# Two token tiles of a gated layer by seven block products in place of eight, behind the layer before it

## The chip, the cores and the metric

The kernel runs on one core of one Trainium2 chip. The metric is the device time of one execution in microseconds, the median of several runs.

## What is computed

Three stages follow one another. A state-space scan over 768 steps (4 batches, 8 heads) gives 3072 tokens of 256 values. Block one is a feed-forward layer of 2048 columns with an ELU. Block two gates two projections of 1024 columns and multiplies the product by two matrices:

```python
x = scan(x, a, B, C).reshape(3072, 256)
h = x @ w_in                                   # 256 -> 2048
x = np.where(h > 0, h, np.exp(np.minimum(h, 0)) - 1) @ w_out   # -> 256
a, b = x @ w1, x @ w2                          # 256 -> 1024 each
out = ((a * b) @ w3) @ w_out2                  # -> 1024 -> 256
```

Inputs and outputs are fp32. The large products run on a rounded fp32 form (float32r): each operand is split into a high part and a low part (what rounding left), and one product is the sum of three matmuls.

## The kernel before

Tokens lie along the free dimension in 6 tiles of 512 (`TT`); features lie on the 128 partitions. The scan works on 24 chunks of 128 steps, four for each tile. Chunks 0 to 3 are done first, step by step; the others come in pairs. `unit_u(k)` computes the products of C with B and the new states of two chunks, `unit_y(k)` their output, which becomes the columns of `xT` for tile k // 4, as high and low part. `at_prep` (L394) is the scan on VectorE that turns decays into the mask L.

Block one goes tile by tile in 8 units of 256 columns. `unit_a(t, n)` makes 12 matmuls into a room of two PSUM banks; then ScalarE takes exp and relu, VectorE joins them with h (L608), and ScalarE and VectorE split the result g into parts. `unit_b(t, n)` multiplies g by `w_out` with 12 matmuls into two accumulators (`acc_b`); for the first four units of tile 0, with plain fp32 words, it needs four matmuls. After the eighth, `split_x2` splits x2 into parts. Tiles 0 to 2 write x2 to DRAM and read it back later (`x2_stored`, `x2_back`).

Block two goes tile by tile in 8 blocks m of 128 columns. `unit_c(t, m)` makes 12 matmuls into a room of two banks, one for each of w1 and w2; ScalarE copies the first (L704), VectorE multiplies it by the second (L706), ScalarE and VectorE split the product p (L713, L122). `unit_d(t, m)` makes 6 matmuls with wp, the product of w3 and the last matrix, which `unit_w` computes beforehand with 192 matmuls of 256 columns.

Every large product is this one:

```python
def mm3(out, whi, wlo, xhi, xlo, first, last, **kw):
    T.matmul(out, wlo, xhi, start=first, stop=False, **kw)
    T.matmul(out, whi, xlo, start=False, stop=False, **kw)
    T.matmul(out, whi, xhi, start=False, stop=last, **kw)
```

Weights come from DRAM as 64-bit words in pieces of 512 KB; a class `Piece` turns each into fp32 with one instruction of ScalarE and two of VectorE, and then into a high part (ScalarE) and a low part (`take_lo`, L122, on VectorE or GpSimd). All loads and stores are issued by SyncE.

The order of all work on every engine is written out by hand: `ORDER` is a string of letters, each of which runs the next waiting step of its kind (`a`, `b`, `c`, `d`, `w`, `u`, `y` are the units; most other letters are single instructions of ScalarE, VectorE or GpSimd), and `in_order` keeps each engine to it. In this string block two of tiles 0, 3, 1, 2 is mixed with the scan and block one of tiles 4 and 5, and the first four chunks have a list of their own, `FIRST_SCAN`. PSUM has 8 banks: three rooms of two banks (`ps_w`) and two accumulators (`ps_a`), which block one and block two share.

Of the kernel before, what the change touches and what calls it, by code (L numbers as in the profile page):

```python
# [35 lines left out]
sbxkrijNsuhKaWkDHDjIKbxtHtiryhIsNbzkzMYYMKXiHahXIjkiaxKrLHsbBxIrLNahsBijbVxRraSsCShCTCTuxCi1brsDahtViaxDtrVVbxsrLyshBiaM  # L36
MzzXYYkbXxLrPKBkHbshIKNiHuhIkaDDjNtbtxirKjsyhkHibMIMzXzYbNYhKkHXiIaKjNkHLIaxKrBkNLHbxIsjrBNKahsSiShwTxTk1jirbKHsfIHFjakh
INRwxKrCNkCjsbHCfIKjFHaCNihIkaxiNjKrkLwxsBrKjbsHfIHFkIuNKhaDtDjNtwkxirKsjaHkfKIHFbkxINKrswhkNjiKyHfIHFbMjzINzYMYbLXhkjNB
iuXhKwkPDjDttbKHfkIHiIyFKwMzMzYXYLXaHLBfHIFRaxBIrLCwxCsrBCshbNCfiFaSkNSThT3jiaxKjkNrKbx1sHrIbNkhsjiHahKNkjiHaxIKrNIHbsjk
xIjbKhkKriHasHIhINbxirsajNkhKHibxIjkrKbHsIhuicDtDtbmnpqcSST3Tcmnpqcmndmncpqdmncpqcmndmndpqcpqcmndmncpqdmncpqdmncpqdmncpq  # L40
oO2cddpqcpmqnmndmndpqcpqcmndmncpqdmndpqcpqdmncpoOq2ymndzMz3YcYpqLMcXmBnXLPdmBncpqRdmnCupCqdDcptDtqcmnymndzMzMYcYXpqXLdLm
BCdnpBqCcpqdmnuOop2cDtDtqdmcnpqamndxrcpsqhdmidpncqpqcmnamnyxrdzMzsdpYhqaYpiqdxLrdBsaOo2axrsbbhixahribxsrbshiahiaxrsbxrsb
hiuhbDiDbttySSTTzczYYcmnpqcmnpqcmncmndmndpqcpqdmnapqdxrcpsqhdmidncpqamnpqaxrsdxhdriaOos2axrsbahixbrxsbhriahsibxrsahibxrs
bhihigGSTeSTEmnmpncmqpnqpqcmnpqdmndpqddccmnpqcmnpqdmndpqddoO
"""
TILES_OF_C = (0, 3, 1, 2, 4, 5)
SPILL = 3
VECTOR_LO = 16
PIECES = [(("w_in", "w_out")[k == "o"], "iiiooioiiiiooooo"[:n].count(k)) for n, k in enumerate("iiiooioiiiiooooo")] + [("wo2", m) for m in range(4)] + [("w3", m) for m in range(16)] + [
    (k, m) for k in ("w2", "w1") for m in range(4)]  # L50

PLAIN = 4

FIRST_SCAN = ["a0", "l0", "a1", "l1", "c0", "u0", "m0", "a2", "l2", "c1", "u1", "p0", "d0", "d1", "a3", "m1", "l3", "y0", "x0",
              "c2", "u2", "d2", "m2", "kjK", "y1", "x1", "c3", "u3", "d3", "HI", "kjK", "m3", "y2", "x2", "h0", "HkjI", "y3",
              "x3", "h1", "n0", "n1", "n2", "n3"]

# [5 lines left out]
def kernel(  # L63
# [27 lines left out]
    ps_w = ctx.enter_context(tc.tile_pool(name="ps_w", bufs=3, space=bass.MemoryType.PSUM))  # L91
    ps_a = ctx.enter_context(tc.tile_pool(name="ps_a", bufs=1, space=bass.MemoryType.PSUM))
# [7 lines left out]
    sel = const.tile([SUB * CPT, CPT, SUB, R], F32R, name="sel")  # L100
# [51 lines left out]
    class Piece:  # L152
# [89 lines left out]
    def cols_of(ws):  # L242
        return lambda i: [w[:, :, i * 256:i * 256 + 256] for w in ws]

    def rows_of(ws):
        return lambda i: [w[:, 2 * i:2 * i + 2] for w in ws]
# [18 lines left out]
    def half_cols(ws, name):  # L265
        def dst(i):
            if not ws:
                ws.extend(four(name, name, [P, F2]))
            return [[w[k][:, i * 256:i * 256 + 256] for k in range(2)] for w in ws]
        return dst  # L270

    def w3_dst(i):
# [42 lines left out]

    def at_first():
# [483 lines left out]
    for p in queue[3:8]:  # L800
        p.load()
# [88 lines left out]
```

## Time and profile before

| | |
|---|---|
| three runs | 548.15, 549.25, 549.32 us (median 549.25) |
| profiled execution | 548.17 us, its span 546.5 us |
| busy | TensorE 531.1, VectorE 341.3, ScalarE 270.2, GpSimd 69.1 us |
| moved | 45.58 MB read, 6.39 MB written |
| mean granted clock of TensorE | 0.999 of 2.4 GHz |

The span runs from the first to the last instruction; the device time has some work around it. In the profile's rows PE is TensorE's matmul, PEld its weight load, DVE is VectorE, ACT ScalarE, POOL GpSimd and SP SyncE. `L394` is a line of the kernel. A row of a stretch gives its start and end, its length, the busy time and the count of instructions of PE, PEld, DVE, ACT and POOL, then the granted clock, the DMA engines' share and GB/s. A row of a timeline gives start, length, engine, line, instruction and count, and in brackets the idle time of that engine before it and what ended it.

### The profile page before, as it was taken

What the parts mean: (1) busy time and instruction counts of PE and PEld (TensorE: products, weight loads), DVE (VectorE), ACT (ScalarE), POOL (GpSimd) and SP (SyncE); (2) the same over time, 40 slices, a digit from 0 to 9 for tenths busy, and PEclk for the clock granted to TensorE, in tenths of its full rate; (3) what the DMA queues carried; (4) which work ended last, traced back from release to release, by engine and by line L of the source; (5) the groups of instructions that cost most, each with busy time, mean ns of one, the idle gap of its engine ahead of it and who ended that gap; (6) DMA issues with size and microseconds to landing.
All of it is one profiled execution on the core that took longest, in us unless ns stands there. A gap on an engine that the chain in (4) does not pass through costs nothing.

```text
span 546.5 us, 10462 instructions
## 1 busy us (share of the span) xinstructions
PE 531.1 (97%) x4420; PEld 427.6 (78%) x4420; DVE 341.3 (62%) x487; ACT 270.2 (49%) x374; POOL 69.1 (13%) x84
## 2 busy tenths in 40 slices
PE   6888899999999999999999999999999999999997
PEld 3646588878888888888888887888888788887885
DVE  6698798999999798874333346644635444454233
ACT  2668666566766358863323232224555234655222
POOL 2420002035452270000000002010000000000000
PEclk9999999999999999999999999999999999999999
DMA  8993652257524639140001025310000000100001
GB/s 300 321 311 122 189 193 79 64 168 229 178 89 143 206 127 340 44 154 1 1 0 38 2 78 175 118 40 0 33 27 0 2 1 1 39 1 0 1 0 40
DMA packets 27167, 52.65 MB, mean 96 GB/s; under 512 B 2192, under 2 KB 10512, under 8 KB 27120
## 3 DMA queue, kind: packets, MB, share of 16 engines
q1 hardware_dynamic: 27120, 51.98, 28.7%
q8 instruction: 35, 0.57, 0.4%
q14 instruction: 12, 0.10, 0.1%
HBM read 45.58 MB, written 6.39 MB: 95 GB/s over the span
## 4 chain that ended last, share of the span: by engine, by line
PE 91%; DMA 3%; ACT 2%; DVE 1%; SPq 1%; issue 1%; DVEq 0%; ACTq 0%
PE ab L290 8%; PE ab L292 8%; PE ab L291 8%; PE acc_b L290 7%; PE h L290 7%; PE acc_b L291 7%; PE h L291 7%; PE h L292 7%; PE acc_b L292 7%; PE acc_d L290 4%; PE acc_d L292 4%; PE acc_d L291 4%; DMA raw_wo<-in_w_out 2%; PE wp L290 1%; PE wp L292 1%; PE wp L291 1%
## 5 line engine op out<-in xcount | busy, mean ns | idle before, releaser
L290 PE MATMUL h<-xTh,w_in_lo 128*128 128x512 f32 (+1 forms) x196 | 76.6, 391 | 2.5 <-DVE w_in_lo L122 2.3
L706 DVE TENSOR_TENSOR pa<-pa,ab 128x512 f32<-128x512 f32 x48 | 32.8, 685 | 71.7 <-ACT pa L704 71.5
L608 DVE SCALAR_TENSOR_TENSOR e<-e,h 128x1024 f32<-128x1024 f32 x44 | 53.5, 1217 | 37.5 <-ACT e L603 37.4
L291 PE MATMUL h<-xTl,w_in_hi 128*128 128x512 f32 (+1 forms) x196 | 75.6, 386 | 0.1
L292 PE MATMUL h<-xTh,w_in_hi 128*128 128x512 f32 (+1 forms) x196 | 75.5, 385 | 0.0
L290 PE MATMUL ab<-x2h,w 128*128 128x512 f32 x192 | 75.2, 392 | 0.0
L291 PE MATMUL ab<-x2l,w 128*128 128x512 f32 x192 | 74.7, 389 | 0.0
L292 PE MATMUL ab<-x2h,w 128*128 128x512 f32 x192 | 74.7, 389 | 0.0
L704 ACT COPY pa<-ab 128x512 f32<-128x512 f32 x48 | 28.1, 588 | 91.5 <-PE ab L292 91.5
L290 PE MATMUL acc_b<-g,w_out_lo 128*128 128x512 f32 x176 | 69.3, 394 | 1.7 <-DVE w_out_lo L122 1.7
L601 ACT ACTIVATE e<-h 128x1024 f32<-128x1024 f32 x48 | 49.3, 1027 | 43.3 <-PE h L292 43.1
L122 DVE TENSOR_TENSOR g<-e,g 128x1024 fp32r<-128x1024 f32 x44 | 56.7, 1288 | 21.3 <-ACT g L612 21.1
L291 PE MATMUL acc_b<-g,w_out_hi 128*128 128x512 f32 x176 | 68.7, 390 | 0.8 <-DVE g L122 0.8
L292 PE MATMUL acc_b<-g,w_out_hi 128*128 128x512 f32 x176 | 68.5, 389 | 0.0
L612 ACT CAST g<-e 128x1024 fp32r<-128x1024 f32 x44 | 46.3, 1053 | 35.4 <-PE acc_b L292 32.6
L603 ACT ACTIVATE e<-e 128x1024 f32<-128x1024 f32 x48 | 50.9, 1061 | 1.1
L122 DVE TENSOR_TENSOR p<-pa,p 128x512 fp32r<-128x512 f32 x48 | 33.6, 700 | 28.3 <-ACT p L713 27.9
L713 ACT CAST p<-pa 128x512 fp32r<-128x512 f32 x48 | 29.8, 622 | 41.0 <-PE acc_d L292 28.1
L400 POOL TENSOR_TENSOR xbc<-xbc,L 128x128 f32<-128x128 f32 x24 | 13.2, 548 | 256.3 <-DVE L L394 240.6
L290 PEld LDWEIGHTS h<-xTh,w_in_lo 128*128 128x128 f32 x196 | 36.8, 188 | 11.2 <-issue 1.8
L292 PEld LDWEIGHTS h<-xTh,w_in_hi 128*128 128x128 f32 x196 | 36.8, 188 | 7.5
L291 PEld LDWEIGHTS h<-xTl,w_in_hi 128*128 128x128 f32 x196 | 36.8, 188 | 7.3 <-DVE xTl L122 0.3
(119 smaller groups left out, 880.5 us busy)
## 6 DMA issues: line engine op xcount, KB each, us to landing
xbc<-in_xc SPq DMA_DIRECT2D x24, 512.0 KB, 5.8
raw_wc<-in_w3t SPq DMA_DIRECT2D x16, 512.0 KB, 4.3
L<-a_cut SPq DMA_DIRECT2D x40, 128.0 KB, 3.5
raw_wi<-in_w_in SPq DMA_DIRECT2D x8, 512.0 KB, 8.2
raw_wo<-in_w_out SPq DMA_DIRECT2D x8, 512.0 KB, 6.7
out_t<-o SPq DMA_DIRECT2D x12, 256.0 KB, 2.0
raw_wq<-in_wo SPq DMA_DIRECT2D x4, 512.0 KB, 7.2
raw_wb<-in_w SPq DMA_DIRECT2D x4, 512.0 KB, 6.2
```

Source lines behind the costliest of these rows:

```text
L122: eng.tensor_tensor(out=lo, in0=raw, in1=hi.bitcast(F32), op=ALU.subtract)
L290: T.matmul(out, wlo, xhi, start=first, stop=False, **kw)
L291: T.matmul(out, whi, xlo, start=False, stop=False, **kw)
L292: T.matmul(out, whi, xhi, start=False, stop=last, **kw)
L400: G.tensor_tensor(out=c["bd"], in0=c["bn"], in1=c["L"][:, :, R - 1:R].to_broadcast([P, NH, N]), op=ALU.mult)
L601: A.activation(e, h, AF.Exp)
L603: A.activation(e, e, AF.Relu, scale=-1.0, bias=1.0)
L608: V.scalar_tensor_tensor(out=gt[t, n] if plain else e, in0=e, scalar=-1.0, in1=h, op0=ALU.mult, op1=ALU.max)
L612: A.copy(g[:, 0], e)
L704: A.copy(e, h[:, 0])
L706: V.tensor_tensor(out=e, in0=e, in1=h[:, 1], op=ALU.mult)
L713: A.copy(p[:, 0], e)
```

## The change

For tiles 2q and 2q+1 together, the two weights and the two halves of the 256 features make a 2 x 2 product of blocks: (w1, w2) by (tile 2q, tile 2q+1). It takes eight block products; the change takes seven, by a form of Strassen's method, with more sums around them.

- The weights' sums are made once for each 256 columns (`gated_sums`, on GpSimd, four sums for each of four pieces) from the fp32 words, and seven operands of each are split into parts (`gated_hi`).
- The tokens' sums are made for each pair (`x2_sums`, `x2_last`, on GpSimd, four of 128x512), and seven operands are split (`operand`: ScalarE, then VectorE). x2 is no longer split at its end but kept whole (`x2_made`); tiles 0 to 3 go to DRAM and back, one tensor each.
- `by_product` issues one of seven products (letters `c e g G E ( )`). Products are added up in four rooms of one bank: two that blocks m take in turn (`p` in the order), `p_A` and `p_E`. A bank is read between two products that are added to it: `kept_1`, `kept_5` and `kept_2` are copies by ScalarE, `sum_11`, `sum_22` and `sum_12` sums by VectorE, `gate_1` and `gate_2` the two gating products on VectorE. `gate_parts` splits p as before.
- Block two of all tiles stands behind the scan and block one in `ORDER`. Its operands use the places of w_in and w_out, its weights the places of the scan's loads. PSUM is handed over in two steps: three rooms of two banks become four rooms of one bank and two accumulators, so block two has four accumulators.
- The first four chunks are now in `ORDER` too, in pairs (`first_cb`, `first_u`, `first_y`); the first half of a unit of tile 0 (`half_a`) is issued ahead for two units. Pieces of w_in and w_out load in another order, and L has four buffers in place of three.

The core of the diff:

```diff
-NMMXKajXkHLjaPxNIBKjNkrLaMxsBXjKrNbkxRXjrsCNjCKbWjCsHCjkjIujKNWkaDKtHkjNIxDaKrtkHsNjbxIKrkLHjysBWIzMazYMhKXkHYKXaxLrPINB
+094AAlU75AlCCACl5Cl5jk5U!KNjkJHKJ6IDN6HjD8N66IQj8D8NDj8kzQNzkYjYzKvzXYjYKaXkHKjvIxMkkarKMkHasxPIrLNbxLBrXsBKXbjRHWNICsMu
...
-TILES_OF_C = (0, 3, 1, 2, 4, 5)
-SPILL = 3
+SPILL = 4
...
-    def unit_c(t, m):
-        h = banks(f"ab{t}_{m}")
-        for k in range(2):
-            c_products(h, t, m, k)
-        yield "m"
-        yield from c_parts(t, m, h)
...
+    def x2_sums(q):
+        (b11, b21), (b12, b22) = ([x2[2 * q + j][:, k] for k in range(2)] for j in range(2))
+        t1, t3 = (att.tile([P, TT], F32, tag="pr", name=f"t{q}_{j}", bufs=2) for j in range(2))
+        G.tensor_tensor(out=t1, in0=b12, in1=b11, op=ALU.subtract)
+        G.tensor_tensor(out=t3, in0=b22, in1=b12, op=ALU.subtract)
+        G.tensor_tensor(out=b12, in0=b22, in1=t1, op=ALU.subtract)
+        later("~", x2_last, q, b11, b21, b12)
+        ops_x[q] = []
+        for n, raw in enumerate((b11, t1, b21, b12, t3, b22, b11)):
+            later("@", operand, q, n, raw)
...
+    def by_product(l, q, m):
+        n = "cegGE()".index(l)
...
+        o = ops_x[q][n]
+        whi, wlo = (v[:, m % 2 * P:m % 2 * P + P] for v in ops_w[m // 2][(0, 4, 1, 5, 6, 2, 3)[n]])
+        ps = rooms["E"] if l in "e(" else rooms["A"] if l == "g" else rooms[m % 2]
+        mm3(ps, whi, wlo, o[:, 0], o[:, 1], l in "ceg", l in "g()", skip_group_check=True)
+        s = mid.setdefault((q, m), {})
+        kind, step = {"c": ("m", kept_1), "e": ("n", kept_5), "g": ("[", sum_11), "G": ("]", kept_2),
+                      "E": ("{", sum_22), "(": ("}", sum_12), ")": (">", gate_1)}[l]
+        later(kind, step, s, q, m)
...
+    def sum_22(s, q, m):
+        V.tensor_tensor(out=s["two"][:, 1], in0=s["p5"], in1=rooms[m % 2], op=ALU.add)
...
+    def gate_1(s, q, m):
+        V.tensor_tensor(out=s["two"][:, 0], in0=s["two"][:, 0], in1=rooms[m % 2], op=ALU.mult)
+        later("p", gate_parts, 2 * q, m, s["two"][:, 0])
```

**The order on TensorE at the start.** Before, where `aw` are the decays of one chunk, `f` its room, and `xbc` its loaded columns:

```order
L382 MATMUL aw_135<-a_hl,sel 128x512 x2
L382 MATMUL aw_140<-a_hl,sel 128x512 x2
L416 MATMUL f_145<-xbc_104 64x128 x8
L451 MATMUL f_145<-xbc_104 32x64 x8
L382 MATMUL aw_165<-a_hl,sel 128x512 x2
L416 MATMUL f_170<-xbc_106 64x128 x8
L451 MATMUL f_170<-xbc_106 32x64 x8
L382 MATMUL aw_193<-a_hl,sel 128x512 x2
```

And in the changed kernel, where two chunks share each room of decays:

```order
L450 MATMUL f_138<-a_hl,sel 128x512 x4
L484 MATMUL f_136<-xbc_111 64x128 x4
L484 MATMUL f_137<-xbc_113 64x128 x4
L484 MATMUL f_136<-xbc_111 64x128 x4
L484 MATMUL f_137<-xbc_113 64x128 x4
L450 MATMUL acc_f<-a_hl,sel 128x512 x4
L484 MATMUL f_138<-xbc_117 64x128 x4
L484 MATMUL acc_f<-xbc_119 64x128 x4
```

The products of C and B (L416 before, L484 now) and those of the states stood chunk by chunk between the decays; now those of two chunks alternate, and all four chunks' come before the states' products.

**The order on VectorE in block two.** Before, where `pa` is the copied w1 half, `ab` the room, and `p` the parts of the gated product:

```order
L706 TENSOR_TENSOR pa_4_3159<-pa_4_3159,ab_4_3093 128x512
L706 TENSOR_TENSOR pa_5_3163<-pa_5_3163,ab_5_3114 128x512
L706 TENSOR_TENSOR pa_6_3172<-pa_6_3172,ab_6_3144 128x512
L122 TENSOR_TENSOR p_4_3181<-pa_4_3159,p_4_3181 128x512
L122 TENSOR_TENSOR p_5_3197<-pa_5_3163,p_5_3197 128x512
L706 TENSOR_TENSOR pa_7_3213<-pa_7_3213,ab_7_3184 128x512
L706 TENSOR_TENSOR pa_0_3222<-pa_0_3222,ab_0_3200 128x512
L122 TENSOR_TENSOR p_6_3238<-pa_6_3172,p_6_3238 128x512
```

And in the changed kernel, in the second pair, for block 3 and part of block 4 (`p_3795` and `p_3796` are the two rooms that blocks take in turn, `p_A` and `p_E` the other two; `p_3843` and `u_3891` are copies that ScalarE kept; `c` holds what becomes the two tiles' gated products; L795 is `sum_22`, L792 `sum_11`, L798 `sum_12`, L801 `gate_2`, L805 `gate_1`, L128 the low part):

```order
L795 TENSOR_TENSOR c_3_4386<-p_3843,p_3796 128x512
L792 TENSOR_TENSOR c_3_4386<-c_3_4386,p_A 128x512
L801 TENSOR_TENSOR c_3_4386<-c_3_4386,u_3891 128x512
L805 TENSOR_TENSOR c_3_4386<-c_3_4386,p_3796 128x512
L128 TENSOR_TENSOR p_3_4469<-c_3_4386,p_3_4469 128x512
L128 TENSOR_TENSOR p_3_4479<-c_3_4386,p_3_4479 128x512
L798 TENSOR_TENSOR u_3891<-u_3891,p_E 128x512
L795 TENSOR_TENSOR c_4_4447<-p_3843,p_3795 128x512
L801 TENSOR_TENSOR c_4_4447<-c_4_4447,u_3891 128x512
L128 TENSOR_TENSOR p_4_4503<-c_4_4447,p_4_4503 128x512
```

One product and one low part for each tile and block, two and two for a pair, became three sums, two products and two low parts for the pair; five of the seven stand in the order between products that TensorE adds to the same rooms.

## Rows read from the trace of the kernel before

**Rows 1.** The page, its first part: busy time, share of the span, instructions.
```profile
PE 531.1 (97%) x4420; PEld 427.6 (78%) x4420; DVE 341.3 (62%) x487; ACT 270.2 (49%) x374; POOL 69.1 (13%) x84
```

**Rows 2.** Stretches of the span; columns as told in the section on the profile.
```profile
0.00:19.30 19.30, 13.68 (x281) 8.36 (x281) 12.55 (x23) 5.87 (x12) 5.86 (x17) 1.00 0.92 327
19.30:80.10 60.80, 55.69 (x621) 38.15 (x622) 50.42 (x80) 42.48 (x61) 8.96 (x17) 1.00 0.71 219
80.10:243.40 163.30, 163.30 (x1533) 136.88 (x1537) 144.65 (x201) 108.69 (x146) 47.75 (x42) 1.00 0.46 152
243.40:323.50 80.10, 80.10 (x420) 65.99 (x428) 30.95 (x48) 24.35 (x41) 0.00 (x0) 1.00 0.04 13
323.50:502.00 178.50, 178.50 (x1411) 146.03 (x1412) 87.53 (x118) 76.57 (x95) 6.54 (x9) 1.00 0.11 37
```

**Rows 3.** The page, its fourth part: the chain that ended last, by engine.
```profile
PE 91%; DMA 3%; ACT 2%; DVE 1%; SPq 1%; issue 1%; DVEq 0%; ACTq 0%
```

**Rows 4.** Timeline of TensorE, 256 to 262 us: first and last of 28 starts.
```profile
255.78 0.39 PE L292 MATMUL ab<-x2h,w 128*128 128x512 f32 x1
...
261.90 0.39 PE L292 MATMUL ab<-x2h,w 128*128 128x512 f32 x1
```

**Rows 5.** Timeline of TensorE, 0 to 75 us: start, length, instruction, idle time before it.
```profile
6.70 1.13 PE L416 MATMUL f<-xbc 32*64 32x128 f32 x16
...
19.29 0.38 PE L290 MATMUL h<-xTh,w_in_lo 128*128 128x256 f32 x1 [0.22 <-POOL w_in_lo L122]
...
24.29 0.40 PE L290 MATMUL h<-xTh,w_in_lo 128*128 128x512 f32 x1
...
28.07 0.47 PE L290 MATMUL h<-xTh,w_in_lo 128*128 128x512 f32 x1 [0.87 <-DVE w_in_lo L122]
...
44.42 0.47 PE L290 MATMUL h<-xTh,w_in_lo 128*128 128x512 f32 x1 [1.38 <-DVE w_in_lo L122]
...
61.48 0.69 PE L416 MATMUL s<-xbc 32*64 32x128 f32 x32
...
67.21 0.50 PE L290 MATMUL acc_b<-g,w_out_lo 128*128 128x512 f32 x1 [1.67 <-DVE w_out_lo L122]
```

**Rows 6.** Timeline at the end of block one and at the last output.
```profile
504.49 1.22 DVE L122 TENSOR_TENSOR g<-e,g 128x1024 fp32r<-128x1024 f32 x1 [1.49 <-ACT g L612]
...
505.76 0.50 PE L291 MATMUL acc_b<-g,w_out_hi 128*128 128x512 f32 x1 [0.76 <-DVE g L122]
...
506.10 0.40 PE L292 MATMUL acc_b<-g,w_out_hi 128*128 128x512 f32 x1
...
542.18 0.39 PE L292 MATMUL acc_d<-p,wp_hi 128*128 128x512 f32 x1
...
542.66 0.59 ACT L736 COPY o<-acc_d 128x512 f32<-128x512 f32 x1 [3.48 <-PE acc_d L292]
```

**Rows 7.** Groups by line and form: count, busy us and mean ns, idle before.
```profile
L122 DVE TENSOR_TENSOR p<-pa,p 128x512 fp32r<-128x512 f32 x48 | 33.6, 700 | 28.3 <-ACT p L713 27.9
...
L706 DVE TENSOR_TENSOR pa<-pa,ab 128x512 f32<-128x512 f32 x48 | 32.8, 685 | 71.7 <-ACT pa L704 71.5
L713 ACT CAST p<-pa 128x512 fp32r<-128x512 f32 x48 | 29.8, 622 | 41.0 <-PE acc_d L292 28.1 <-DVE pa L706 10.7 <-DVE p L122 2.2
L704 ACT COPY pa<-ab 128x512 f32<-128x512 f32 x48 | 28.1, 588 | 91.5 <-PE ab L292 91.5
```

**Rows 8.** Timeline of VectorE and GpSimd, 128 to 134 us.
```profile
128.78 1.21 DVE L394 TENSOR_TENSOR_SCAN L<-L,eye 128x512 f32<-128x512 f32 x1
...
130.45 1.63 POOL L122 TENSOR_TENSOR w<-raw_wc,w 128x512 fp32r<-128x512 f32 x1 [2.49 <-ACT w L194]
...
130.83 2.33 DVE L394 TENSOR_TENSOR_SCAN L<-L,eye 128x512 f32<-128x512 f32 x1
...
132.04 1.34 POOL L400 TENSOR_TENSOR xbc<-xbc,L 128x128 f32<-128x128 f32 x1
...
133.09 1.19 DVE L608 SCALAR_TENSOR_TENSOR e<-e,h 128x1024 f32<-128x1024 f32 x1
```

More of the change, by code (lines that the diff above doesn't have):

```diff
@@ L199, in los @@
                 take_lo(self.lo, l, w, h)
-    w_in_s = pair([P, 2, F1], "w_in")
-    w_out_s = pair([P, F1 // P, DM], "w_out")
+    NA, NC = F1 // P // 2, F2 // P
+    w_in_s, w_out_s = ([wts.tile([P, 2, 2, 256], F32R, tag=f"{name}{n}", name=f"{name}{n}") for n in range(NA)]
+                       for name in ("w_in", "w_out"))
     wp_s = pair([P, F2 // P, DM], "wp")
-    wo2_s, w1_s, w2_s = [], [], []
+    wo2_s = []
     w3_st = {}
@@ L240, in blocks, with parts_at, acc_of @@
                 for f in range(0, F2, P) for i in range(0, F2, 512)]
[L242 to L246, printed above, removed]
+    def parts_at(ws):
+        return lambda i: [ws[i][:, p] for p in range(2)]
+    acc_f = ps_f.tile([P, 2, TT], F32, name="acc_f")
+    accs = []
+    def acc_of(i, other=0):
+        if not accs:
+            pool = sums(two, "ps_a", 1, "right")
+            accs.extend(pool.tile([P, TT], F32, name=f"acc{j}") for j in range(2))
+        return accs[2 * other + i]
     words = []
@@ L263, in wo2_dst, with slot @@
         return [w[i // 2][:, 2 * (i % 2):2 * (i % 2) + 2] for w in wo2_s]
[L265 to L270, printed above, removed]
+    slots = []
+    def slot(n):
+        if n // 2 >= len(slots):
+            j = len(slots)
+            if j < 8:
+                new = [wts.tile([P, 4, 256], F32R, tag=f"w{2 - j // 4}_{j % 4}", name=f"s{j}")]
+            elif j < 12:
+                new = [att.tile([P, 4, 256], F32R, tag="xbc", name=f"s{j}", bufs=4)]
+            else:
+                both = [att.tile([P, 2, 256], F32R, tag="L", name=f"s{j}_{k}", bufs=4) for k in range(2)]
+                slots.append(both)
+                return slot(n)
+            slots.append([new[0][:, :2], new[0][:, 2:]])
+            return slot(n)
+        return slots[n // 2][n % 2]
@@ L695, in ended_c @@
[L695 to L708 removed]
+        nc.sync.dma_start(x2_dram[t], x2.pop(t))
+    x2_dram = tc.dram_tile([SPILL, P, 2, TT], F32, name="x2_dram")
@@ new lines, in x2_last, with operand @@
+    def x2_last(q, b11, b21, t2):
+        G.tensor_tensor(out=b11, in0=b21, in1=t2, op=ALU.subtract)
+    def operand(q, n, raw):
+        o = wts.tile([P, 2, TT], F32R, tag=f"{('w_in', 'w_out')[q % 2]}{n}", name=f"x{q}_{n}")
+        ops_x[q].append(o)
+        A.copy(o[:, 0], raw)
+        yield "#"
+        take_lo(V, o[:, 1], raw, o[:, 0])
+    rooms = {}
+    mid = {}
+    def by_product(l, q, m):
+        n = "cegGE()".index(l)
+        if not rooms:
+            pool = sums(six, "ps_c", 1, "left")
+            rooms.update({k: pool.tile([P, TT], F32, name=f"p_{k}") for k in (0, 1, "A", "E")})
+            accs.extend(pool.tile([P, TT], F32, name=f"acc{j}") for j in (2, 3))
+        o = ops_x[q][n]
[6 more added lines that the diff above has]
+        later(kind, step, s, q, m)
+        if l in "E(":
+            s["ready"] = s.get("ready", 0) + 1
+            if s["ready"] == 2:
+                later("<", gate_2, s, q, m)
@@ new lines, in halves_of, with kept_1, kept_5, kept_2 @@
+    def halves_of(name, tag, m):
+        if name not in rooms:
+            rooms[name] = wts.tile([P, 2, TT], F32, tag=tag, name=name)
+        return rooms[name][:, m % 2]
+    def kept_1(s, q, m):
+        s["two"] = tmp(f"c{q}_{m}")
+        A.copy(s["two"][:, 0], rooms[m % 2])
+    def kept_5(s, q, m):
+        s["p5"] = halves_of("p5", f"w_in{NA - 1}", m)
+        A.copy(s["p5"], rooms["E"])
+    def kept_2(s, q, m):
+        s["u2"] = halves_of("u2", f"w_out{NA - 1}", m)
+        A.copy(s["u2"], rooms[m % 2])
@@ new lines, in unit_d, with copied @@
+        for i, kind, cs in ((0, "o", slice(0, TT)), (1, "O", slice(0, TT // 2)), (1, "o", slice(TT // 2, TT))):
+            later(kind, copied, t, i, tmp(f"o{t}_{kind}{i}")[:, 0, cs], cs, A if kind == "O" else nc.sync)
+    copies = []
+    def copied(t, i, o, cs, queue):
+        (A.copy if i == 1 and cs.start == 0 else V.tensor_copy)(o, acc_of(i, t % 2)[:, cs])
+        if queue:
+            stored(queue, t, i, o, cs)
+            return
+        copies.append((nc.sync, t, i, o, cs))
+        if len(copies) == 2:
+            later("2", lambda: [stored(*copies.pop(0)) for _ in range(2)] and None)
```

346 lines of the change are left out of this document (169 added, 177 removed).

## Prediction

> **What bounds the kernel now.** I read the busy shares first, then the stretches, then the chain of waits, and only then single instructions. TensorE is busy 531.1 of 546.5 us, VectorE 341.3, ScalarE 270.2, GpSimd 69.1 [rows 1]. A busy share is an average, so the stretches decide: from 80.1 us to 502 us TensorE is busy in every microsecond (163.30 of 163.30, 80.10 of 80.10, 178.50 of 178.50), at a granted clock of 1.00, which is its 2.4 GHz level; before 80.1 us it is idle for 5.6 and 5.1 us [rows 2]. VectorE takes 144.65 of 163.3 us (89%) in the middle of block one and 30.95 of 80.1 us (39%) where only block two runs [rows 2]. So another engine's work costs nothing as long as TensorE doesn't have to wait for it, and this holds at 89%. The chain of waits says the same: 91% of it is TensorE [rows 3]. In a dense stretch 27 matmuls of 512 columns go by between the starts at 255.78 and 261.90 us: 6.12/27 = 0.2267 us each [rows 4]. The 0.39 us that a row prints is not its cost, since matmuls overlap.
>
> **The change, part by part.**
>
> *Products taken away.* For two token tiles and one 128-column block m of block two, the kernel issued 2 tiles x 2 weights x 2 halves x 3 parts = 24 matmuls; now 7 products x 3 = 21. There are 3 pairs x 8 blocks: 504 in place of 576. The order of instructions bears this out (288 into the two alternating banks, 72 into p_A, 144 into p_E). 72 x 0.2267 = **-16.3 us**, all of it on the path, since TensorE had no gap there. The 288 matmuls of the output product stay. Nothing here can take this away; what follows can only add to it or eat it.
>
> *The start.* The first four chunks are now issued in pairs. One chunk alone takes 1.13 us for its 16 products of C and B, a pair takes 0.69 us for 32 [rows 5]. The first w_in product stands at 19.29 us [rows 5]; I keep that time, because the same four scans, the same masked products and one weight piece are ahead of it on VectorE's queue in either order. What changes is what follows: units 0 and 1 of block one now come with nothing of the scan between them and would both be done at 19.3 + 2 x 2.72 = 24.7 us, where the second of them ended at 24.29 + 12 x 0.2267 = 27.0 [rows 5]. That is 2.3 us. From there to 80.1 us the old TensorE is idle for 5.1 us [rows 2], of which 0.87, 1.38 and 1.67 are waits for VectorE's low parts [rows 5], and it loses about 1 us more in first matmuls that start slowly after a wait (0.34 in place of 0.23 [rows 6]). Pieces of w_in and w_out are now loaded in turn, so the low parts of w_out can come sooner. All of it gone would be -8 us, none of it 0. VectorE's 63 us of work in the first 80.1 [rows 2] would then have to fit into 72, so some waits will stay. I take **-5 us**; a load that comes late could cost up to 3 us instead.
>
> *Block one without block two between.* Three u units, four y units and tiles 4 and 5 of block one move ahead of all of block two, so VectorE gets no relief until about 340 us. Its work outside the gating is at most 341.3 - 33.6 - 32.8 = 275 us [rows 1, 7]; the 16 new low parts of the summed weights and the operands that are made early are at most 30 instructions, 21 us at 0.70. 296 of 340 us is 87%, no more than the 89% under which TensorE never waited [rows 2, 7]. Cost 0. The cover is VectorE's 13%; were it gone, each missing microsecond would stand on the path. The x2 traffic falls from 6 stores and 6 loads to 4 and 4. The eight loads of w1 and w2 keep their number and now wait on SyncE's queue behind the last chunks of the scan; nothing of block one is queued behind them that is due soon. Also 0.
>
> *A gap that goes.* At 505.76 us TensorE resumes after 0.76 us without work, on the last g of tile 5 [rows 6]. Now 12 us of other units are issued between unit 7 of the last tile and its second product: **-0.8 us**.
>
> *Gating in block two.* For each pair and m ScalarE had 4 instructions (2 copies, 2 casts), VectorE 4. Now ScalarE has 5 and VectorE 7, all 128x512. VectorE: 24 x 7 x 0.70 = 118 us, with the operands of the later pairs about 130 of 180 us, or 72% [rows 7]. Share is not the risk; the banks are. A product's bank is added to again after it has been read, so 168 product groups of 0.68 us each wait for a copy or a sum. The trace has no such wait; the nearest rows price its parts. A reader starts 0.25 us after the last matmul's slot (542.18 + 0.23 to 542.66) and TensorE resumes 0.05 us after the vector instruction (504.49 + 1.22 to 505.76) [rows 6]. So a round trip is 0.25 + 0.59 + 0.05 = 0.89 us over ScalarE and 0.99 over VectorE, if nothing is queued ahead. In the new order I counted what TensorE is given meanwhile: 0.68 us in 4 places, 1.36 us in 44, 2.05 us or more in the other 116. The 4 lose up to 0.3 us each. The 44 lose nothing with a free engine, and 0.2 to 0.3 us with one instruction ahead. I walked the second pair by hand, from the first product of block 4 to the outputs of block 3, by these prices: VectorE's four sums and products of block 3 end 5.7 us after that start, its two low parts at 6.4 and 7.6, and the output products that need them are due at 8.2 and 9.5. No wait there. I take 1.2 us for the 4, a third of the 44 at 0.2 us, and nothing for the chain to the output product, about **+4 us** in all. Bounds: 0.5 us (all but the 4 covered) and 12 us (every one of the 48 at 0.25).
>
> *GpSimd's new work.* 16 sums of weights and 12 of x2 tiles. In the old trace a VectorE scan of 1.21 us takes 2.33 us when a GpSimd subtraction of 1.63 us began just before it: it ends 1.1 us after that subtraction does, as if it had begun there [rows 8]. The sums of weights lie in block one, where VectorE has the slack. Of the 12 x2 sums 8 lie where block one ends and the first pair begins; what they could hold up there is rival B, and in the sum I take 0. The Trainium skill (the page "SBUF — State Buffer", section "Who interferes with whom") makes this a rule against the change: a VectorE instruction with both inputs in SBUF and a GpSimd instruction that reads SBUF shut each other out for the whole instruction. The trace agrees (2.33 in place of 1.21 us [rows 8]). If the rule struck at every added x2 sum, the sum would be B's 536 us; without it, 531.
>
> **Sum.** 546.5 - 16.3 - 5 - 0.8 + 4 = 528.4 us of span. The profiled execution took 548.17 us, 1.67 more than its span: 530.1. It stands 1.1 us under the median of the three runs (549.25), so on that scale **531 us**. A difference under 0.2% (1.1 us) can't be told from none here.
>
> **Rivals.**
>
> *A. The gating falls behind (10%).* If an instruction stands ahead on VectorE at most of the 44 places, and the late output products then hold the p tiles, the waits cost 12 to 19 us and nearly all of the 16.3 is given back: 539 to 546 us. For it: four one-bank rooms where three two-bank rooms were, and 72% load in place of 39%. Against it: the walk above, and 116 of the 164 covers being over 2 us.
>
> *B. The lock on the switch (10%).* Eight GpSimd sums at 1.1 us hold VectorE back by up to 9 us while it must also make the last g tiles and 14 operands; TensorE has 12 us of other work there, so some 5 us come through: 536 us. For it: the scan that was held up [rows 8]. Against it: an instruction that reads its second input from PSUM shows no such stretch (L608 at 133.09, 1.19 us beside a GpSimd product [rows 8]), and the four GpSimd sums of one pair needn't all meet a low part.
>
> *C. Slower than before (6%).* Without any wait in block two the sum is 531 - 4 = 527 us. To pass 549.25 block two would have to wait 22 us, 0.93 us per pair and m. A wait with 1.36 us of cover over VectorE loses 0.99 + 0.69k - 1.36 us with k instructions ahead; with two such places per pair and m, k = 1.2 on average is the point from which the change loses. Then VectorE's fixed order, not TensorE, would set the pace, with all 7 instructions of a block strung on the bank's chain. The walk shows k near 0 in the one place tried, so I hold this improbable.
>
> That the change doesn't do what it says is shut out by the order of instructions: 504 matmuls stand there in place of 576. No difference within 0.2% (2%) is only the narrow strip between A and C.
>
> **How the numbers follow.** The forecast has 72%. Its own range takes the start and the waits to their bounds: 546.5 - 16.3 - 8 - 0.8 + 0.5 + 2.8 = 525 us, and 546.5 - 16.3 - 0 - 0.8 + 8 + 2.8 = 540 (waits at two thirds of their bound, as both ends together are unlikely; 2.8 is 1.67 + 1.1). B lies in it. With one us at each end I give 524 to 541; most of A, and C, stay outside. Faster: 72 + 10 + 10 = 92%; same 2%; slower 6%.
>
> **What would show it.** TensorE dense from about 75 us to the end, block two in about 184 us (792 x 0.2267 = 179.5, and 4 of waits), its last stretch with VectorE near 70% and no more than 5 us of TensorE idle. The second unit of block one ends near 25 us. The forecast is wrong if TensorE idles over 8 us in block two on sums or copies of p banks (A, C), if VectorE low parts of 1.5 to 2.3 us stand on the chain at the switch (B), or if block one itself shows TensorE waiting for VectorE after 80 us.

## The result and the profile after

The changed kernel took **529.31 us** (median of 4 runs, 528.42 to 529.65) beside 548.70 us for the kernel before (4 runs, 547.28 to 549.32): a ratio of 0.9648, 95% interval 0.9623 to 0.9672. The forecast was 531.0. The profiled execution took 528.42 us with a span of 526.7, so the span shrank by 546.5 - 526.7 = 19.8 us.

The page of the changed kernel, first part (compare [rows 1]), then the chain's shares (compare [rows 3]):

```profile
PE 512.8 (97%) x4360; PEld 414.9 (79%) x4360; DVE 398.1 (76%) x569; ACT 297.0 (56%) x419; POOL 106.1 (20%) x112
...
PE 95%; DMA 2%; SPq 1%; issue 1%; ACT 1%; DVE 0%; DVEq 0%; ACTq 0%
```

TensorE lost 18.3 us of busy time and still fills 97% of a shorter span, 95% of the chain in place of 91%. VectorE grew by 57 us and ScalarE by 27, and neither has a larger share of the chain than before (VectorE 0%, ScalarE 1%).

Stretches of the changed kernel, cut at the first w_in products, at the place that answers to 80.1 us of before (sixteen units done in both: ten first products and six second ones before, nine and seven now, and where they differ each is 12 matmuls of 512 columns), at the first copy of block two (334.3) and at the last matmul (columns as in [rows 2]):

```profile
0.00:19.30 19.30, 10.71 (x222) 6.54 (x223) 13.44 (x25) 7.81 (x15) 8.79 (x23) 1.00 0.92 326
19.30:76.10 56.80, 56.26 (x691) 41.13 (x691) 48.46 (x79) 37.93 (x54) 7.28 (x9) 1.00 0.68 208
76.10:240.00 163.90, 163.90 (x1886) 136.34 (x1885) 138.84 (x186) 104.19 (x130) 55.73 (x49) 1.00 0.44 135
240.00:334.30 94.30, 94.30 (x742) 76.91 (x743) 71.86 (x91) 64.90 (x79) 28.45 (x28) 1.00 0.23 74
334.30:430.00 95.70, 95.60 (x421) 78.47 (x420) 65.68 (x100) 45.63 (x81) 5.85 (x5) 1.00 0.03 12
430.00:521.90 91.90, 91.85 (x405) 75.56 (x403) 59.17 (x90) 36.20 (x62) 0.00 (x0) 1.00 0.04 13
521.90:526.70 4.80, 0.19 (x1) 0.00 (x0) 0.67 (x2) 0.37 (x1) 0.00 (x0) 0.95 0.55 198
```

Read the second column against the first. Between 19.3 and 76.1 us TensorE is idle for 0.54 us, all of it the end of a stop that the next rows show, where it had 5.1; in all of block two, with VectorE at 64 to 69%, for 0.15 us by this count. As much work is done 80.03 - 76.1 = 3.9 us earlier. The first row shows a loss: the 222 matmuls that are through by 19.3 us were 281 before.

The timeline of TensorE at the start (compare [rows 5]):

```profile
15.54 1.28 PE L553 MATMUL f<-L,xbc 64*32 64x64 f32 x64 [0.62 <-DVE L L491]
16.74 0.64 PE L561 MATMUL f<-xbc,st 32*32 32x64 f32 x22
19.84 0.44 PE L561 MATMUL f<-xbc,st 32*32 32x64 f32 x10 [2.46 <-issue]
...
21.93 0.58 PE L345 MATMUL h<-xTh,w_in 128*128 128x256 f32 x1
22.31 0.41 PE L346 MATMUL h<-xTl,w_in 128*128 128x256 f32 x1
22.53 0.41 PE L347 MATMUL h<-xTh,w_in 128*128 128x256 f32 x1
...
24.60 0.28 PE L345 MATMUL h<-xTh,w_in 128*128 128x256 f32 x1
24.72 0.28 PE L346 MATMUL h<-xTl,w_in 128*128 128x256 f32 x1
```

In the middle of a run of 32 small products TensorE stops for 2.46 us and the trace names nobody it waited for. The first w_in product stands at 21.93 us, where the forecast kept 19.3, and the first matmuls after it are 0.21 us apart before they close up to 0.12. The kernel before had such a stop too, a shorter one, and its fourth chunk's outputs (the last two rows) came behind the first w_in product at 19.29 us; now those of all four chunks come ahead of it. The timeline of TensorE in the kernel before:

```profile
18.05 0.26 PE L451 MATMUL f<-xbc 64*32 64x64 f32 x5 [0.97 <-issue]
...
20.74 0.46 PE L484 MATMUL f<-L,xbc 64*32 64x64 f32 x32 [0.48 <-ACT st L467]
21.13 0.43 PE L492 MATMUL f<-xbc,st 32*32 32x64 f32 x16
```

The timeline of TensorE at the two longest waits of block two:

```profile
381.50 0.39 PE L347 MATMUL p<-x,s 128*128 128x512 f32 x1
381.99 0.50 PE L345 MATMUL p<-x,s 128*128 128x512 f32 x1
...
493.44 0.39 PE L347 MATMUL p_E<-x,s 128*128 128x512 f32 x1
493.88 0.50 PE L345 MATMUL p<-x,s 128*128 128x512 f32 x1
```

The starts are 0.49 and 0.44 us apart where a slot is 0.2267: 0.26 and 0.21 us lost, and some 0.1 us more before the next start each time. Both have one product (0.68 us) of cover, and so has the third and last, 0.16 us at 367.30: three of the four such places. Over all starts of block two (333.1 to 521.7 us) the distances add up to 1.1 us more than the slots.

### The profile page after: what moved, and what is told of

Same layout as the page of the kernel before. It is cut to its first block, busy times and chain, and to the rows that moved or that the text cites. A ratio compares the mean times of both kernels' runs of the same rounds, so it can differ in the third digit from the quotient of the medians.

```text
span 526.7 us, 10487 instructions
## 1 busy us (share of the span) xinstructions
PE 512.8 (97%) x4360; PEld 414.9 (79%) x4360; DVE 398.1 (76%) x569; ACT 297.0 (56%) x419; POOL 106.1 (20%) x112
## 4 chain that ended last, share of the span: by engine, by line
PE 95%; DMA 2%; SPq 1%; issue 1%; ACT 1%; DVE 0%; DVEq 0%; ACTq 0%
PE acc L345 12%; PE acc L346 12%; PE acc L347 12%; PE h L345 9%; PE h L346 8%; PE h L347 8%; PE p L345 4%; PE p L346 4%; PE p L347 4%; PE acc L700 3%; PE p_E L345 2%; PE p_E L346 2%; PE p_E L347 2%; DMA raw_wi<-in_w_in 2%; PE y L553 1%; PE y L561 1%
## 5 line engine op out<-in xcount | busy, mean ns | idle before, releaser
L345 PE MATMUL h<-xTh,w_in 128*128 128x512 f32 (+1 forms) x200 | 77.9, 389 | 0.0
L346 PE MATMUL h<-xTl,w_in 128*128 128x512 f32 (+1 forms) x200 | 76.8, 384 | 0.0
L347 PE MATMUL h<-xTh,w_in 128*128 128x512 f32 (+1 forms) x200 | 76.6, 383 | 0.0
L345 PE MATMUL acc<-g,w_out 128*128 128x512 f32 x176 | 70.3, 399 | 0.0
L347 PE MATMUL acc<-g,w_out 128*128 128x512 f32 x176 | 68.6, 390 | 0.0
L346 PE MATMUL acc<-g,w_out 128*128 128x512 f32 x176 | 68.6, 390 | 0.0
L128 DVE TENSOR_TENSOR g<-e,g 128x1024 fp32r<-128x1024 f32 x44 | 57.1, 1298 | 13.2 <-ACT g L682 13.1
L813 ACT CAST p<-c 128x512 fp32r<-128x512 f32 x48 | 29.8, 622 | 47.1 <-DVE c L801 29.0
L345 PEld LDWEIGHTS h<-xTh,w_in 128*128 128x128 f32 x200 | 38.2, 191 | 7.8 <-issue 0.2
L347 PEld LDWEIGHTS h<-xTh,w_in 128*128 128x128 f32 x200 | 38.2, 191 | 7.4
L346 PEld LDWEIGHTS h<-xTl,w_in 128*128 128x128 f32 x200 | 38.2, 191 | 6.8
L128 DVE TENSOR_TENSOR p<-c,p 128x512 fp32r<-128x512 f32 x48 | 33.0, 688 | 13.8 <-ACT p L813 13.4
L345 PEld LDWEIGHTS acc<-g,w_out 128*128 128x128 f32 x176 | 33.0, 188 | 7.7 <-issue 0.2
L347 PEld LDWEIGHTS acc<-g,w_out 128*128 128x128 f32 x176 | 33.0, 188 | 7.1
L346 PEld LDWEIGHTS acc<-g,w_out 128*128 128x128 f32 x176 | 33.1, 188 | 6.7 <-issue 0.2
L345 PE MATMUL p<-x,s 128*128 128x512 f32 x96 | 37.7, 392 | 0.2
L345 PE MATMUL acc<-p,wp_lo 128*128 128x512 f32 x96 | 37.4, 389 | 0.0
L346 PE MATMUL p<-x,s 128*128 128x512 f32 x96 | 37.4, 389 | 0.0
```

The source lines that it names most:

```text
L128: eng.tensor_tensor(out=lo, in0=raw, in1=hi.bitcast(F32), op=ALU.subtract)
L813: A.copy(p[:, 0], e)
```

## Experiments

Each was an edit of the changed kernel; its 529.31 us are the base. The kernel before, measured again with each group of runs, had medians from 548.2 to 549.5 us, so a difference of about 1 us between groups shows nothing by itself.

### Eight products again

```diff
         mm3(ps, whi, wlo, o[:, 0], o[:, 1], l in "ceg", l in "g()", skip_group_check=True)
+        if l == "g":
+            mm3(ps, whi, wlo, o[:, 0], o[:, 1], l in "ceg", l in "g()", skip_group_check=True)
```

> The product 'g' of each pair and block m is issued twice into the same bank, the second time starting over, so the output does not change and there are again 576 product matmuls. Theory (block two is bound by TensorE, the saving is matmul slots): 72 x 0.2267 = +16.3 us on the changed kernel, less at most the 1 us of idle that block two has, so +15.3 to +16.3: about 545 us, and the rest of the change is then worth 3 to 4 us against the kernel before. Rival (the order of VectorE's and ScalarE's instructions sets the pace in block two, TensorE is stretched to it): under +8 us. Rival (the start and block one gave most of it): also under +8 us.

Measured: 545.03 us (544.54 to 546.04), **+15.7**; the span grew from 526.7 to 543.3, by 16.6. Against the kernel before the ratio is 0.9939 (0.9919 to 0.9959). The waits of block two stayed the same to the hundredth (1.1 us over the slots, now for 72 more matmuls). So matmul slots are what the change saves, and all the rest of it, new order, start and switch together, is worth 3.4 us (548.45 us for the kernel before in this group).

### How much room VectorE has

```diff
     def gate_1(s, q, m):
+        for _ in range(2):
+            V.tensor_tensor(out=begun.rearrange("p k i -> p (k i)"), in0=s["two"][:, 0], in1=eye.rearrange("p h i -> p (h i)"), op=ALU.add)
         V.tensor_tensor(out=s["two"][:, 0], in0=s["two"][:, 0], in1=rooms[m % 2], op=ALU.mult)
```

Once, twice (as shown) and three times:

> One added VectorE instruction of 128x512 (about 0.7 us, its result is not used) right ahead of the last product of tile one's gating, per pair and block m: 24 in all, 16.6 us of VectorE. Theory (VectorE has room at the banks): hidden but for a few waits, 0 to +4 us. Rival (VectorE's order is on the edge, one more instruction ahead of a bank's reader costs its whole length): +12 to +17 us.

> Two such instructions per pair and block m: 48 in all, 33 us of VectorE, 9 in place of 7 beside the low parts of the operands, about 6.3 of 7.5 us per block. Theory: partly hidden, +2 to +10 us. Rival (on the edge): +28 to +34 us.

> Three such instructions per pair and block m: 72 in all, 50 us of VectorE, 10 per block or about 7.0 of 7.5 us before the operands of the next pair. Theory: the room is used up, +12 to +25 us. Rival (on the edge): +45 to +50 us. If it stays under +10 us, the waits at the banks were never near, and the 4 us of waits in the forecast's sum had no ground.

| added per pair and m | time, us | against the changed kernel | TensorE's starts in block two over the slots, us |
|---|---|---|---|
| 0 | 529.31 | | 1.1 |
| 1 | 532.56 | +3.3 | 4.6 |
| 2 | 542.53 | +13.2 | 14.3 |
| 3 | 558.08 | +28.8 | 31.2 |

The first is mostly hidden, as the theory had it. The second costs 10 us of the 16.6 that 24 instructions take, and the third 15.5. So both larger runs lie above what my theory gave them (10 and 25 at most): the room is a little over one instruction per pair and m, not two. With three the ratio to before is 1.0173 (1.0142 to 1.0205): slower, by less than 2%. Its profiled execution (559.74 us, the slowest of four) lost some 2.5 of the 31.2 us by the clock and not by waits: behind a wait of 3.1 us matmuls of 512 columns stood 0.427 us apart for some 5 us, at a granted clock of 0.50, the 1.2 GHz level:

```profile
392.00:397.70 5.70, 5.70 (x14) 4.45 (x15) 1.87 (x3) 1.87 (x4) 1.28 (x1) 0.50 0.01 3
```

All waits by TensorE of the kernel with two added, block two (what waited, for whom; us in total, times, longest us), and below it the stretches of that kernel and of the one with three (334 to 430 and 430 to 521.9 us):

```profile
PE p L345 <- DVE c L807: 7.4, 9, 2.3
PE p_E L345 <- ACT p L785: 0.5, 1, 0.5
PE p_E L345 <- DVE u L798: 0.5, 1, 0.5
```

```profile
334.00:430.00 96.00, 90.63 (x387) 71.38 (x386) 72.13 (x111) 42.73 (x74) 6.48 (x5) 1.00 0.03 12
430.00:521.90 91.90, 88.69 (x384) 71.09 (x383) 71.56 (x109) 36.60 (x63) 0.00 (x0) 1.00 0.03 12
```

```profile
334.00:430.00 96.00, 85.69 (x350) 66.51 (x349) 73.62 (x113) 40.95 (x70) 6.45 (x5) 0.96 0.02 6
430.00:521.90 91.90, 83.12 (x353) 65.33 (x352) 73.29 (x112) 31.49 (x54) 0.00 (x0) 1.00 0.05 18
```

The waits add up to 8.4 us and the starts lose 14.3, since a row counts idle time only from the printed end of the matmul before it (0.39 us after its start, where a slot is 0.2267) and the start behind a wait is slow. L807 is the product gate_1, the one behind the added instructions: it holds the bank that the first product of the next block but one wants (two rooms, taken in turn). That is rival C's mechanism, and VectorE is busy for only 75 to 80% (72.13 of 96, 73.29 of 91.9) when it sets the pace, since its fixed order makes it wait in turn. With two added, from 334 to 521.9 us, it waits 25.6 us for the products that its three sums read and 8.7 us for ScalarE's part of p. The room is measured at this one place, ahead of gate_1. Four of VectorE's seven instructions, the three sums and gate_1, read a bank (gate_2 reads none), and what an instruction ahead of a sum costs was not tried.

### GpSimd's sums left out

```diff
-        G.tensor_tensor(out=t1, in0=b12, in1=b11, op=ALU.subtract)
-        G.tensor_tensor(out=t3, in0=b22, in1=b12, op=ALU.subtract)
-        G.tensor_tensor(out=b12, in0=b22, in1=t1, op=ALU.subtract)
...
-        for n, raw in enumerate((b11, t1, b21, b12, t3, b22, b11)):
+        for n, raw in enumerate((b11, b12, b21, b12, b22, b22, b11)):
...
-        G.tensor_tensor(out=b11, in0=b21, in1=t2, op=ALU.subtract)
+        return None
```

> The twelve GpSimd sums of x2 tiles are left out; the operands of block two are made from the plain x2 tiles, so its products are those of other numbers and the output is not the reference's. The 16 sums of weights stay. Theory (they hold no VectorE instruction that TensorE waits for): 0, within 0.6 us. Rival (GpSimd's sums hold VectorE back at the switch, the forecast's rival B): -2 to -5 us, and the low parts at L128 between 300 and 345 us get shorter and TensorE closes gaps there.

Measured: 529.08 us (528.45 to 529.84), the same within 0.3 us. The low parts of the operands between 296 and 346 us (durations in ns, least, median, most), in the changed kernel and without the sums:

```profile
L128 DVE TENSOR_TENSOR x<-x2b,x x10: 682/684/1783, 300.6 to 341.4; 128x512 fp32r<-128x512 f32 x10
```

```profile
L128 DVE TENSOR_TENSOR x<-x2b,x x14: 684/687/705, 299.4 to 341.2; 128x512 fp32r<-128x512 f32 x14
```

Beside GpSimd one of them took 1783 ns, without it none over 705. So an instruction is held up, and TensorE, dense from 240 to 334.3 us either way, never notices. Rival B's mechanism is there and its price is 0.

### The start: pairing

```diff
-        cb_products(*((k, ck[k]["room"][0]) for k in ks))
+        for k in ks:
+            cb_products((k, ck[k]["room"][0]))
...
-        y_products(*((k, ck[k]["room"][2]) for k in ks))
+        for k in ks:
+            y_products((k, ck[k]["room"][2]))
```

> The products of C and B and those of the scan's output are issued chunk by chunk for the first four chunks, not chunk pair by chunk pair; everything else of the change stays. Theory (the pairing, not the new order of loads and low parts, brings the early part forward): the four C-B products cost 1.13 us each in place of 0.69 per pair, so up to 3 us at the start: +1 to +3.5 us. Rival (the start is paced by loads and by what TensorE waits for at 17.4 us): 0 to +0.5 us.

Measured: 529.40 us (529.01 to 529.54), +0.1: by the time, the rival. The timeline of TensorE is less clear:

```profile
20.00 0.58 PE L561 MATMUL f<-xbc,st 32*32 32x64 f32 x10 [2.26 <-issue]
...
22.89 0.58 PE L345 MATMUL h<-xTh,w_in 128*128 128x256 f32 x1
```

The stop is there too. What small matmuls cost before it is covered by TensorE's waits (it begins at 17.74 us, 17.38 with pairs), but behind it they take 2.89 us in place of 2.09, the first w_in product stands 0.95 us later and the last matmul 0.85 us later (522.55 for 521.70). So pairing may be worth up to 0.9 us; the times don't resolve it.

### The start: order of the weight loads

The piece order is shown in part; the moved steps of the order table are left out.

```diff
...
-PIECES = [(("w_in", "w_out")[k == "o"], "iioioiiooiioiooo"[:n].count(k)) for n, k in enumerate("iioioiiooiioiooo")]
+PIECES = [(("w_in", "w_out")[k == "o"], "iiiooioiiiiooooo"[:n].count(k)) for n, k in enumerate("iiiooioiiiiooooo")]
...
```

> The weight pieces of block one are loaded in the order of the kernel before (three of w_in, two of w_out, one of w_in, one of w_out, five of w_in, the rest of w_out) in place of in turn; four steps of the order table stand up to 41 places later so that nothing is used before it is there; everything else of the change stays. Theory (the load order is what makes the low parts and joined words come in time and took away the early waits of 0.87, 1.38 and 1.67 us): waits for weights come back between 22 and 80 us, 1 to 4 us in all, and the time grows by as much. Rival (it was the order of VectorE's steps and the place of block two's work, not the loads): within 0.6 us, and no wait over 0.5 us before 80 us.

Measured: 531.64 us (531.08 to 534.54), +2.3, ratio to before 0.9694 (0.9659 to 0.9729). That interval touches the changed kernel's own, so the trace has to carry the argument. The timeline of TensorE, all its idle times from 22 to 100 us:

```profile
43.38 0.47 PE L345 MATMUL h<-xTh,w_in 128*128 128x512 f32 x1 [0.44 <-DVE w_in L128]
61.92 0.50 PE L345 MATMUL acc<-g,w_out 128*128 128x512 f32 x1 [1.39 <-DVE w_out L128]
```

In the changed kernel there is none. Two of the old kind of wait come back, for low parts of w_in and w_out, 1.8 us in all; with the slow starts behind them the last matmul comes 2.7 us later (524.39 for 521.70), and nearly all of that arises at these two places. So the load order accounts for 1.8 of the 5.1 us of early idle time; that the order of VectorE's steps took away the rest is argued, not shown.

### The start: what TensorE stops for at 17.4 us

First suspicion: its next instructions come by DMA and are stuck behind 1.5 MB of weights. Two runs load the last one or two of these pieces after 20 us; the diffs show that stretch of the order table (N issues a load, X a load of a chunk, j is ScalarE's step on a piece).

```diff
-D8N66IQj8D8NDj8kzQNzkYjYzKvzXYjYKaXkHKjvIx
+D8N66IQj8D8NDj8kzQzkYjYzKvzXYjYKaXNkHKjvIx
```

> The eighth weight piece (w_out's third, 512 KB) is loaded behind the two chunks of the scan that SyncE issues at 20.3 us, not at 11.7 us; about 1.3 us of transfers go out of the stretch before 19.5 us. Theory (TensorE's 2.46 us without work at 17.4 us is its next block of instructions behind a full DMA queue, since the trace names no one it waited for): the gap shrinks by up to 1.3 us and the kernel by 0.5 to 1.3 us. Rival (the gap has nothing to do with the transfers): gap 2.4 to 2.5 us, time within 0.5 us, or more if the piece comes late.

```diff
-D8N66IQj8D8NDj8kzQNzkYjYzKvzXYjYKaXkHKjvIx
+D8N66IQj8D8Dj8kzQzkYjYzKvzXNYYKaXNkHKjjvIx
```

> The seventh and the eighth weight piece (1 MB) are loaded one behind each of the two chunks that SyncE issues at 20.3 us, and ScalarE's step on the seventh stands a little later. Theory (instructions of TensorE behind the queue): 2.6 us of transfers are out of the way, so the 2.46 us gap nearly goes, -1 to -2.4 us if the pieces are still in time. Rival (nothing to do with the transfers): gap 2.4 to 2.5 us, time the same or, with a late piece, up to +2 us.

Measured: 530.11 us (+0.8, no more than groups differ) and 532.31 us (530.18 to 533.41, +3.0), with stops of 2.62 and 2.45 us. With both pieces away the DMA engines stand nearly empty through the stop, as their view from 17.8 to 20.1 us shows, and TensorE resumes no sooner:

```profile
DMA  1120000000000000020002000200100000000000
GB/s 36 71 107 0 0 0 0 0 0 0 0 0 0 0 0 0 0 36 0 0 0 36 0 0 0 36 0 0 36 0 0 0 0 0 0 0 0 0 0 0
DMA packets 15, 0.02 MB, mean 9 GB/s; under 512 B 5, under 2 KB 5, under 8 KB 15
```

```profile
20.17 0.44 PE L561 MATMUL f<-xbc,st 32*32 32x64 f32 x10 [2.45 <-issue]
```

So traffic during the stop isn't its cause (traffic before 17 us was not taken away), and a piece that comes later is waited for: in the second run ScalarE stands 3.03 us until the w_out piece of 30.1 us is there, and TensorE 2.09 us for the g behind it, at 34.1 us.

Second suspicion: a count of instructions.

```diff
     def first_cb(*ks):
...
+        if ks[0]:
+            cb_products(*((k, ck[k]["room"][0]) for k in range(2)))
         cb_products(*((k, ck[k]["room"][0]) for k in ks))
```

> The 32 small products of C and B of the first two chunks are issued a second time right behind the first four chunks' a sums, where TensorE is idle (10.2 to 12.7 us); same values into the same places. Nothing else changes. Theory (TensorE stops at 17.4 us because it has come to the end of the instructions that have been brought in, at a fixed count of instructions): the stop comes 32 matmuls earlier in the program, inside the products at L553 in place of L561, and, if bringing in the next block starts at a count as well, it is over earlier by up to 1.4 us, so the first w_in product stands at 20.5 to 21.8 us and the time is 0 to -1.4 us. Rival (the stop belongs to what L561 reads or writes): it stays in front of the same product at L561 with 2.4 to 2.6 us, and the time stays within 0.5 us.

Measured: 532.20 us (530.83 to 533.69), +2.9. The timeline of TensorE in that kernel:

```profile
15.49 1.24 PE L553 MATMUL f<-L,xbc 64*32 64x64 f32 x54 [0.62 <-DVE L L491]
...
18.89 0.45 PE L553 MATMUL f<-L,xbc 64*32 64x64 f32 x10 [2.16 <-issue]
...
22.63 0.26 PE L561 MATMUL f<-xbc,st 32*32 32x64 f32 x1 [1.00 <-issue]
...
23.00 0.58 PE L345 MATMUL h<-xTh,w_in 128*128 128x256 f32 x1
...
28.29 0.41 PE L345 MATMUL h<-xTh,w_in 128*128 128x256 f32 x1
28.50 0.41 PE L346 MATMUL h<-xTl,w_in 128*128 128x256 f32 x1
...
29.02 0.28 PE L346 MATMUL h<-xTl,w_in 128*128 128x256 f32 x1
29.13 0.28 PE L347 MATMUL h<-xTh,w_in 128*128 128x256 f32 x1
```

The theory's place is right and its price wrong. The stop moved 32 matmuls up in the program, from L561 into L553: it comes after the 222nd matmul in both kernels, and in the one without pairs. It ended a microsecond sooner. But a second stop came 128 matmuls later, and w_in's first product at 23.00 us, 1.07 us late. Behind it 27 matmuls of 256 columns stood some 0.21 us apart, up to 28.9 us, where twelve did in the changed kernel: 15 x 0.093 = 1.4 us more. Together that is the 2.5 us by which the last matmul comes later (524.17 for 521.70). Both stops fit the one queue that the page calls instruction. The DMA view of the changed kernel from 17.2 to 17.4 us, and of this one from 16.2 to 16.4 us:

```profile
q8 instruction: 1, 0.02, 32.8%
```

```profile
q8 instruction: 1, 0.02, 32.7%
```

One packet each. In the traces they begin at 17.35 and 16.25 us, and TensorE resumes 2.49 and 2.64 us behind that; the second packet of the padded kernel begins at 20.00 us, and TensorE resumes 2.63 us later. In the kernel before the packet came at 15.52 us and TensorE resumed at 18.05, again 2.53 us. The stop is what is left of these 2.5 us when TensorE has nothing more to do: it was through at 17.38 us in the changed kernel, 0.03 us behind the packet's start, and at 17.08 us in the kernel before, 1.56 us behind it. Over the whole program this queue moves 34 packets in the changed kernel for 4360 matmuls and as many weight loads, one for 128. So the small matmuls, some 50 to the microsecond, would run through 128 before the next ones are in. That is a reading of these times; no run changed the packets themselves.

### The tail, alone and with the repetition

```diff
-            later(kind, copied, t, i, tmp(f"o{t}_{kind}{i}")[:, 0, cs], cs, A if kind == "O" else nc.sync)
+            room = act.tile([P, 2, TT], F32, tag="p", name=f"o{t}_last") if cs.start else tmp(f"o{t}_{kind}{i}")
+            later(kind, copied, t, i, room[:, 0, cs], cs, A if kind == "O" else nc.sync)
```

> VectorE's last copy of the output, half of the last tile's second part, goes to a buffer of another group (one that held a p tile) in place of the one whose store is under way; nothing else changes. Theory: the copy waits 1.52 us for the store of 2.16 us that still reads its buffer, and its own store ends the program, so -1.0 to -1.5 us. Rival (the program's end hangs on the store of the other half, issued just before): 0 to -0.4 us.

> That repetition and the other buffer for the last copy, together. Theory (they act at the two ends of the program and do not touch each other): the sum of the two alone, -1.1 us of the last copy and 0 to -1.4 us of the start, 526.8 to 528.2 us. Rival (what is won at the start is lost in waits for weights before 80 us): -1.1 us alone or less.

VectorE's last copy in the changed kernel, and with the other buffer:

```profile
523.66 0.42 DVE L836 COPY o_o<-acc 128x256 f32<-128x256 f32 x1 [1.52 <-DMA out_t<-o]
```

```profile
522.71 0.42 DVE L837 COPY o_last<-acc 128x256 f32<-128x256 f32 x1 [0.39 <-ACT o_O L837]
```

The wait on a store is gone, the copy starts 0.95 us sooner although this run's last matmul was 0.18 us later, and the time is **528.21 us** (527.74 to 529.23), ratio to before 0.9613 (0.9594 to 0.9632): the lowest median here, 1.1 us below the changed kernel. The ranges of the two overlap, and so do the intervals; the trace is the better evidence: from the last matmul to the end of the span it takes 4.14 us, 4.99 in the changed kernel. With the repetition added it took 531.43 us (529.32 to 534.93), slower than either theory had it: the repetition costs 3.2 us here too.

## Why the prediction was right, point by point

- **Products, -16.3.** Right: +15.7 on the time and +16.6 on the span when the 72 matmuls are put back. This term is nearly all of the change, and nothing took it away.
- **The start, -5.** Came to -3.9. The step that failed is "I keep that time": the first w_in product slid from 19.29 to 21.93 us, by 2.64 us. Of these 1.49 are the longer stop in which TensorE seems to have run out of instructions (2.46 us, 0.97 before), 0.30 its later begin, and 0.85 what comes between the stop and that product. There the reason that I gave was wrong: the fourth chunk's masked product and its 48 matmuls were not ahead of the first w_in product before (they ran at 20.74 us) and are now. The second unit of block one ended at 28.9 us, not at 24.7, and not at 27.0 as before: 1.9 us lost where I had 2.3 won. From there to the place of as much work 5.8 us were won, nearly all of the 6.1 that the forecast had as the most: all idle time after 21.93 us went, where I had said that some waits would stay, and the loads in turn are part of it (1.8 us of waits return without them). That the term came near -5 is luck: two errors against each other.
- **Block one without block two between, 0.** Right: 163.90 of 163.90 and 94.30 of 94.30 us busy up to the switch, with VectorE at 85% (138.84 of 163.9).
- **The gap at tile 5, -0.8.** Gone as said; the list of TensorE's waits names nothing from 22 us on. By starts it was worth 1.1 us: the start at 505.76 us stood 1.20 behind the one before it (504.56) and the next one 0.34 behind that [rows 6], where a slot is 0.2267.
- **Waits of the gating, +4.** Mis-sized: 1.1. The four places of 0.68 us were priced right (1.2 forecast, 0.96 at three of them, the slow start behind each included). The 44 of 1.36 us cost nothing, where I had let a third of them lose 0.2 us; that no instruction stood ahead of their readers when it mattered is the likely reason. The added instructions show how near that was at gate_1: one more per pair and m and its places begin to lose.
- **GpSimd's lock, 0.** Right, for a stronger reason than I gave: no low part at the switch has TensorE waiting.
- **Rival C's point** was 22 us of waits in block two. It lies between two added instructions (14.3) and three (31.2), and the kernel crosses from 1.1% faster to 1.7% slower between them.

The terms, with the products at their slots, add up: 546.5 - 16.3 - 3.9 - 0.8 + 1.1 = 526.6, beside a span of 526.7. It is not quite so good: the gap was worth 0.3 more, and the sum leaves out that the tail from the last matmul to the end grew by 0.7 us, from 4.27 to 4.99, which the forecast had at nothing. With both it is 527.0. The forecast's 528.4 was too high by the waits (2.9) and too low by the start (1.1).

## What to carry to other kernels

Where TensorE is dense, price a cut in matmuls by slots and believe it; then ask how many instructions of the readers' engine fit before their order sets the pace. Here that was a little over one per pair and block, ahead of one reader, at a busy share that still read 64 to 69%; the share alone would have promised three. And when many tiny matmuls come in a row, count them: the stop put down to "issue" at a fixed count wasn't cured here by moving data; pairing them changed nothing that the times resolve, and repeating them made it worse.

## What was not expected of the hardware

- TensorE seems to stop for lack of instructions: after the 222nd matmul (with as many weight loads) in the changed kernel and the padded one, and again 128 matmuls later in the padded one. A packet of the instruction queue begins 2.4 to 2.7 us ahead of each resumption, with the DMA engines full or nearly empty. What starts the first packet (15.5 us before, 17.35 after) stays open.
- After the 2.46 us stop twelve matmuls of 256 columns stood 0.213 us apart, 1.2 columns per ns, the pace of the 1.2 GHz level, though the granted clock of that stretch reads 1.00; then 0.12 us. That is 12 x 0.093 = 1.1 us more. In the kernel with three added instructions the same pace (512 columns in 0.427 us) stands where the granted clock does read 0.50. Weight loads of those matmuls read 0.33 us in place of 0.19. The Trainium skill (page "TensorE: Matmul & The Clock Gate", section "Seeing it yourself") warns that recorded clock events have been seen to be unreliable on this chip; these rows agree. The row of that stretch, the clock third from the end:

```profile
21.90:24.50 2.60, 2.60 (x20) 2.57 (x13) 2.12 (x6) 1.90 (x5) 0.00 (x0) 1.00 0.99 385
```
